# Twelve small loads around the last weights of a decode step, and w4 in two pieces instead of eight, begun after the last projection

## The chip, the cores and the metric

The kernel runs on one core of one Trainium2 chip. The metric is device time in microseconds (us) of one execution; lower is better. Times inside an execution are counted from its first instruction.

## The reference

One token goes through two blocks and the results are added. Block A is attention with 32 query heads over 4 key/value heads of 65536 cached keys each. Block B is a small MLP.

```python
xn = layernorm(x)
# A: 134 MB of cache are read once
q = xn @ wq                                    # 1024 x 4096
o = softmax(q @ K^T * 128**-0.5) @ V           # per head, K and V: [4, 65536, 128]
A = o @ wo                                     # 4096 x 1024
# B
h  = gelu(layernorm(xn) @ w1);  x1 = xn + shifted(h) @ w2
B  = x1 + gelu(layernorm(x1) @ w3) @ w4        # w4: 3584 x 1024
out = x + A + B
```

All is bf16. Some 170 MB have to come from memory for very little arithmetic, so the kernel is a race against its own loads. The shifts leave only zeros at a sequence length of one.

## The kernel before

Loads go through one queue (SyncE) into three slots of 64 KB per partition, in a fixed order. The last four are the last K tile, wo, the last V tile, and w4. A slot is loaded again when its user is done.

```python
SLOTS = 3
W4_PIECES = (6, 5, 6, 4, 3, 2, 1, 1)         # in chunks of 128 rows; 28 in all
...
for u in range(NU):
    if u == NU - 1: stream += [("K", u), "wo", ("V", u)]
    else:           stream += [("K", u), ("V", u)]
stream.append("w4")
...
elif it == "w4":
    w4_v = B_w4.rearrange("(m c) n -> m c n", c=FC)
    c0 = 0
    for n in W4_PIECES:
        go(out=t[:, c0 * D:(c0 + n) * D], in_=w4_v[:, c0:c0 + n, :].rearrange("p c n -> p (c n)"))
        c0 += n
```

Everything that forms the output row is added up in one PSUM tile, `psB`. Its two halves of 512 columns sit in two column groups of the PE array, so two matmuls (a pair) run at a time: both start within 7 ns and take 0.38 us each at full clock. The end of the program is:

```python
def compute_w4(lo, hi):
    for c in range(lo, hi):
        for j in range(2):                    # one pair for each chunk
            row_acc(j, hT[:, c:c + 1], wt[:, D * c + 512 * j:D * c + 512 * (j + 1)])
...
for g in range(HKV - 1): project(g)           # o @ wo for three heads groups
add_projection()                              # ... copied (o_rows) and added into psB
compute_v(NU - 1)                             # last P @ V; then on DVE: og, ol; PE: pm_e; DVE: oT
early = sum(W4_PIECES[:2])                    # 11 chunks
compute_w4(0, early)
project(HKV - 1)                              # 8 pairs, needs oT
compute_w4(early, FC)
# out_t <- psB, store
```

Between the last V matmul and `oT` there is a chain of small steps on DVE with one matmul (`pm_e`) in it. Apart from four matmuls that add `o_rows`, PE has nothing else to do there but the early w4 matmuls.

## Time and profile before

| | before |
|---|---|
| time, median of 2 runs | 402.12 us |
| span of the profiled run | 400.3 us |
| last V tile landed | 379.3 us |
| last piece of w4 landed | 396.7 us |
| PE done with psB | 397.2 us |

The page of the kernel before, its span, the busy time of the engines, its load queue (packets, MB, share of 16 DMA engines) and what was read:

```profile
span 400.3 us, 2563 instructions
...
PE 236.0 (59%) x1348; PEld 45.2 (11%) x854; DVE 208.9 (52%) x154; ACT 27.3 (7%) x35; POOL 5.3 (1%) x28
...
q1 hardware_dynamic: 4560, 169.87, 98.6%
...
HBM read 169.87 MB, written 0.00 MB: 424 GB/s over the span
```

The DMA engines are busy all the time; no compute engine is. The chain of waits of the kernel before, its end (start us, us, what):

```profile
379.33 17.39 DMA big<-in_B_w_dram
396.73 0.04 issue
396.77 0.40 PE psB L191 x2
397.17 0.02 issue
397.19 0.58 ACT out_t L455
```

After the last byte of w4 only one pair of matmuls is left. The timeline of PE in the kernel before shows why (start us, us, engine, line, op, out<-in, shapes, count, then in brackets the idle time and what ended it; rows of other engines are left out):

```profile
386.21 2.30 PE L191 MATMUL psB<-big,hT 128*1 128x512 bf16 x10
...
388.44 0.80 PE L403 MATMUL pm_e<-ol,sel8big 128*128 128x129 f32 x2
...
389.17 1.50 PE L191 MATMUL psB<-big,hT 128*1 128x512 bf16 x12
...
390.51 1.89 PE L191 MATMUL psB<-big,oT 128*1 128x512 bf16 x16
...
392.23 2.97 PE L191 MATMUL psB<-big,hT 128*1 128x512 bf16 x26
395.47 1.03 PE L191 MATMUL psB<-big,hT 128*1 128x512 bf16 x6 [0.27 <-DMA big<-in_B_w_dram]
...
396.77 0.38 PE L191 MATMUL psB<-big,hT 128*1 128x512 bf16 x2 [0.27 <-DMA big<-in_B_w_dram]
```

The first two rows of w4 (10 and 12 matmuls) are the early ones; 16 with oT are the last projection. From 395.47 PE waits for the loads, so it has caught up. Ten matmuls from 386.21 take 2.30 us; 26 later take 2.97 us. The cause is PE's granted clock, in the busy times by stretch (us; busy time and count of PE, PEld, DVE, ACT, POOL; granted clock; DMA share and GB/s):

```profile
384.00:386.00 2.00, 0.88 (x4) 0.09 (x4) 1.97 (x3) 0.00 (x0) 0.00 (x0) 0.97 1.03 426
386.00:389.30 3.30, 3.30 (x16) 1.08 (x16) 1.52 (x3) 0.00 (x0) 0.00 (x0) 0.50 0.99 417
389.30:393.00 3.70, 3.70 (x36) 1.44 (x34) 0.91 (x4) 0.00 (x0) 0.00 (x0) 1.00 1.00 412
```

PE was idle for 1.33 us before its four `o_rows` matmuls at 385.12; the clock records show 0.50 from 385.88 to 389.29. So the early matmuls themselves run at half clock, and the last projection, from 390.51, has the full clock. A pair starts every 0.425 us at 0.50 and every 0.2155 us at 1.00. The clock records change in steps of 3.41 us.

### The profile page before, as it was taken

The numbers are of one execution on the slowest core, as the hardware profiler recorded it, in microseconds if no ns is written. First come the engines' busy times: TensorE is split into PE (matmuls) and PEld (weight loads), VectorE is DVE, ScalarE is ACT, GpSimd is POOL, SyncE is SP. The second block draws the span as 40 slices with busy tenths as digits, with TensorE's granted clock in tenths as the row PEclk, the third lists the DMA queues.
The fourth block names the chain that finished last, engine by engine and source line by source line (L and its number), as shares of the span: only waits on it lengthen the run. The fifth ranks groups of instructions, "written<-read, shape, count | busy, mean of one in ns | idle before, by whom it ended". The sixth has DMA issues, their size and how long they took to land.

```text
span 400.3 us, 2563 instructions
## 1 busy us (share of the span) xinstructions
PE 236.0 (59%) x1348; PEld 45.2 (11%) x854; DVE 208.9 (52%) x154; ACT 27.3 (7%) x35; POOL 5.3 (1%) x28
## 2 busy tenths in 40 slices
PE   0561960591678247922965195629453946594986
PEld 0210000010200110011102010201020102000222
DVE  1601010965196549644953994279349931975040
ACT  1001010003000200020002000100100020002000
POOL 2000000000000000000000000000000000000000
PEclk9995795597669666978796789568865986697989
DMA  9998999999999999999999999999999998999895
GB/s 419 419 453 371 435 471 458 426 419 419 421 426 465 452 426 414 426 426 432 445 460 426 419 426 419 447 439 452 426 421 426 432 445 385 432 481 426 385 417 201
DMA packets 4575, 170.01 MB, mean 425 GB/s; under 512 B 467, under 2 KB 469, under 8 KB 982
## 3 DMA queue, kind: packets, MB, share of 16 engines
q1 hardware_dynamic: 4560, 169.87, 98.6%
q8 instruction: 8, 0.13, 0.1%
q14 instruction: 1, 0.01, 0.0%
q10 hardware_dynamic: 6, 0.00, 0.0%
HBM read 169.87 MB, written 0.00 MB: 424 GB/s over the span
## 4 chain that ended last, share of the span: by engine, by line
DMA 51%; DVE 26%; PE 16%; ACT 3%; another core or an unknown queue 2%; issue 1%; DVEq 0%; ACTq 0%
DMA big<-in_A_k_cache_dram 31%; DVE big L327 19%; DMA big<-in_A_v_cache_dram 10%; PE sc L332 8%; PE oacc L382 6%; DMA big<-in_A_wq_dram 6%; DMA big<-in_B_w_dram 4%; DVE p_sb L353 3%; DVE mx L337 3%; ACT p_sb L350 3%; PE psq L257 2%; DVE m L341 0%; PE pm_mx L339 0%; PE pm_mx L346 0%
## 5 line engine op out<-in xcount | busy, mean ns | idle before, releaser
L332 PE MATMUL sc<-big,qdiag 128*128 128x512 bf16 x512 | 129.5, 414 | 62.7 <-DVE big L327 57.2
L327 DVE STREAM_TRANSPOSE big<-big 128x4096 f32<-128x4096 f32 x32 | 139.4, 4413 | 49.4 <-DMA big<-in_A_k_cache_dram 49.4
L382 PE MATMUL oacc<-big,p_sb 128*32 128x512 bf16 x512 | 46.9, 539 | 34.5 <-DVE p_sb L353 34.5
L337 DVE TENSOR_REDUCE mx<-sc 128x1 f32<-128x2048 f32 x8 | 18.3, 2291 | 30.0 <-PE sc L332 30.0
L332 PEld LDWEIGHTS <-qdiag 128*128 128x128 bf16 x128 | 13.2, 103 | 174.7 <-issue 145.9
L350 ACT ACTIVATE p_sb<-sc,nball 128x2048 bf16<-128x2048 f32 x8 | 15.7, 1967 | 217.8 <-DVE nball L348 217.8
L353 DVE STREAM_TRANSPOSE p_sb<-p_sb 128x2048 bf16<-128x2048 bf16 x8 | 18.5, 2311 | 18.0 <-ACT p_sb L350 18.0
L382 PEld LDWEIGHTS <-p_sb 128*32 128x32 bf16 x512 | 17.1, 129 | 61.0 <-DVE p_sb L353 35.1
L257 PE MATMUL psh<-big,ln_rep_b 128*32 128x512 bf16 (+1 forms) x64 | 12.4, 941 | 7.6 <-DMA big<-in_B_w_dram 7.6
L421 PE MATMUL o_acc<-big,oT 128*1 128x512 bf16 x48 | 12.8, 437 | 2.4 <-ACT p_sb L350 2.4
L339 PE MATMUL pm_mx<-ident_f,mx 128*1 128x128 f32 x8 | 2.2, 273 | 19.1 <-DVE mx L337 19.1
L296 DVE STREAM_TRANSPOSE h_row<-h_row 128x896 bf16<-128x896 bf16 x1 | 1.1, 1111 | 20.8 <-ACT h_row L295 20.8
L391 DVE SCALAR_TENSOR_TENSOR og<-oacc,wb,og 128x512 f32<-128x512 f32 x4 | 3.0, 746 | 16.7 <-PE oacc L382 16.7
L191 PE MATMUL psB<-big,hT 128*1 128x512 bf16 x56 | 8.1, 424 | 0.6 <-DMA big<-in_B_w_dram 0.5
L427 DVE COPY o_rows<-o_acc 1x1024 f32<-1x1024 f32 x1 | 1.2, 1211 | 13.6 <-PE oacc L382 13.6
L205 PE MATMUL pm_ln<-ln_rowsum_a,ones_f 128*128 128x1 f32 x2 | 0.6, 348 | 12.5 <-DVE ln_rowsum_a L203 12.5
L403 PE MATMUL pm_e<-ol,sel8big 128*128 128x129 f32 x8 | 2.8, 446 | 7.9 <-DVE ol L402 7.9
L257 PE MATMUL psq<-big,ln_rep_a 128*32 128x512 bf16 x64 | 6.2, 573 | 1.5 <-DMA big<-in_A_wq_dram 1.5
L281 POOL COPY qdiag<-qx 32x32 bf16<-32x32 bf16 x16 | 3.2, 203 | 279.5 <-PE sc L332 249.6
L196 DVE STREAM_TRANSPOSE x_t<-x_row 32x256 bf16<-32x256 bf16 x4 | 2.5, 616 | 8.1 <-DMA x_row<-in_A_x_dram 8.0
L269 DVE CAST q_row<-psq 128x512 bf16<-128x512 f32 x1 | 0.7, 691 | 8.4 <-PE psq L257 8.4
L346 PE MATMUL pm_mx<-ident_f,rep 1*128 1x1 f32 x8 | 1.8, 223 | 5.0 <-DVE rep L343 5.0
(95 smaller groups left out, 73.2 us busy)
## 6 DMA issues: line engine op xcount, KB each, us to landing
big<-in_A_wo_dram SPq DMA_DIRECT2D x1, 8192.0 KB, 36.0
big<-in_B_w_dram SPq DMA_DIRECT2D x1, 7168.0 KB, 38.3
big<-in_B_w_dram SPq DMA_DIRECT2D x2, 2048.0 KB, 46.3
big<-in_B_w_dram SPq DMA_DIRECT2D x2, 1536.0 KB, 27.3
big<-in_B_w_dram SPq DMA_DIRECT2D x1, 1280.0 KB, 24.1
big<-in_B_w_dram SPq DMA_DIRECT2D x1, 1024.0 KB
big<-in_B_w_dram SPq DMA_DIRECT2D x1, 768.0 KB, 30.7
big<-in_B_w_dram SPq DMA_DIRECT2D x1, 512.0 KB, 31.5
```

The lines of the kernel that those rows point to most:

```text
L191: nc.tensor.matmul(psB[32 * j:32 * j + lhsT.shape[1], :], lhsT=lhsT, rhs=rhs, start=start, stop=False, tile_position=(0, 32 * j), skip_gro ...
L257: nc.tensor.matmul(acc[32 * q:32 * q + 32, i, 0:n], lhsT=rep[:, c, :], rhs=cols(c, i, q), start=(c == 0), stop=(c == DC - 1), tile_positio ...
L281: nc.gpsimd.tensor_copy(out=qdiag[at, LEAD:].rearrange("p (x c) -> p x c", x=4)[:, :, 32 * a:32 * a + 8], in_=qx[at, :, 8 * g:8 * g + 8])
L327: nc.vector.transpose(out=words, in_=words)
L332: nc.tensor.matmul(sc[:, e, :], lhsT=qdiag[:, c0:c0 + P], rhs=cols[:, s, e, :, b2, :, r], start=(s == 0 and b2 == 0 and r == 0), stop=(s = ...
L337: nc.vector.reduce_max(out=mx[:], in_=sc[:].rearrange("p e n -> p (e n)"), axis=AX.X)
L350: nc.scalar.activation(out=p_sb[:], in_=sc[:], func=ACTF.Exp, bias=nball[:, b:b + 1], scale=SCALE, accum_out=group["lall"][:, b:b + 1])
L353: nc.vector.transpose(out=flat, in_=flat)
L382: nc.tensor.matmul(oacc[32 * q:32 * (q + 1), :], lhsT=pT[:, e, 32 * t:32 * (t + 1)], rhs=vt[:, :, e, t, :], start=(e == 0 and t < 4), stop ...
L391: nc.vector.scalar_tensor_tensor(out=og[:], in0=oacc[:], scalar=wb[:, 1:2], in1=og[:], op0=ALU.mult, op1=ALU.add)
L403: nc.tensor.matmul(pe[:, 0:DH + 1], lhsT=sel8big[:], rhs=ol[:], start=True, stop=True)
L421: nc.tensor.matmul(tail["rows"][0:1, h2, :], lhsT=oT[g][:, j:j + 1], rhs=wt[:, g, j, 512 * h2:512 * (h2 + 1)], start=(g == 0 and j == 0), ...
```

## The change

Six small loads stand behind wo, and six between two pieces of w4. Each has k rows of 16k bytes, with its own k, into a small tile that nobody reads. No two have the same size, so they can be told apart in the packet records; we take them for marks that show how far each DMA engine has come. With that w4 comes in two pieces, 20 and 8 chunks, and none of it is worked on before the last projection.

```diff
-W4_PIECES = (6, 5, 6, 4, 3, 2, 1, 1)
+W4_PIECES = (20, 8)
+FIRST_MARKS = (3, 6, 8, 10, 13, 15)
+MARKS = (4, 5, 7, 9, 11, 14)
...
+            if it == "wo":
+                marks, m0 = ogpool.tile([P, D], BF16, name="marks", tag="og"), 0
+                self.marks = marks
+                for k in FIRST_MARKS:
+                    go(out=marks[0:k, m0:m0 + 8 * k], in_=A_wo[0:k, 0:8 * k])
+                    m0 += 8 * k
...
                 for n in W4_PIECES:
                     go(...)
+                    if c0 == 0:
+                        marks, m0 = self.marks, 440
+                        for k in MARKS:
+                            go(out=marks[0:k, m0:m0 + 8 * k], in_=A_wo[0:k, 0:8 * k])
+                            m0 += 8 * k
                     c0 += n
...
-    early = sum(W4_PIECES[:2])
+    early = 0
```

So three things change at once: the small loads, the pieces, and the order on PE.

More of the change, by code (lines that the diff above doesn't have):

```diff
@@ L153, in load @@
                     go(out=t[:, c0 * D:(c0 + n) * D], in_=w4_v[:, c0:c0 + n, :].rearrange("p c n -> p (c n)"))
+                    if c0 == 0:
[3 more added lines that the diff above has]
+                            m0 += 8 * k
                     c0 += n
-            else:
+            elif it[0] in ("K", "V"):
                 kind, i = it
```

## The prediction

> **What bounds the kernel now.** The loads. The page gives a mean of 425 GB/s over the 400.3 us span, one queue busy for 98.6% of 16 engines, HBM read 169.87 MB; PE is busy 59%, DVE 52%. The chain of waits ends with a V-cache load that lands at 379.3, 17.39 us of loading w4, then 0.40 us of two psB matmuls, 0.58 us of ACT out_t and the store. w4 comes in eight pieces, the last of one chunk, so almost no PE work follows the last byte. PE has caught up with the loads by then.
>
> **Removed.** Six of the eight w4 loads. The bytes stay. In the trace's packet records a 2048-byte packet takes 84 ns and a 65536-byte one 2418 ns, so by estimate each packet costs about 9 ns beyond its bytes; 54 packets fewer per DMA engine save about 0.5 us before the last w4 byte lands.
>
> **Added.** Twelve loads of k rows and 16k bytes. [...] Estimate: 20 to 30 ns each[...].  Each takes about 0.35 us to issue on SP, off the path. In the changed build, DMA semaphores are reused every eight loads: the last V load now waits for K to land (near 340.5 instead of 338.8), the second w4 piece for V (379.3). At both moments another load still has over 10 us to run, so I expect no bubble.
>
> **Moved: the part that matters.** PE did 11 chunks of w4 before the last projection. Now the order on PE is: V matmuls (end 383.8), o_rows, pm_e, 16 projection matmuls, 40 matmuls of w4 when 20 chunks have landed (estimate 379.3 + 17.4 x 20/28 = 391.7), 16 for the last 8 chunks. pm_e no longer queues behind w4, so oT is ready near 389.5 (390.2 before). PE idles for most of 384 to 389.5 and its granted clock will be 0.50 there; the timeline shows a pair of these matmuls 0.43 us apart at 0.50 and 0.216 us at 1.00. [...] this trace's clock records step in 3.41 us. So the projection's 8 pairs start cold, and the clock returns between 391.3 and 396. From 389.5, 36 pairs then end between 398.2 and 400.4, mean about 399.3, against 397.17 before. Even without cold clock, 16 matmuls (1.7 us) follow the last landing instead of two (0.4).
>
> **On the critical path:** +1.0 to +3.3 us in the tail, about +2.1; loads -0.3 to +0.1. Predicted 404.2 us, 403.1 to 405.5 (8 in 10); faster by over 2%: 0.01, within 2%: 0.97, slower by over 2%: 0.02.
>
> **What would show it.** Right: the rate stays near 425 GB/s until the last w4 byte, which lands within 0.5 us of 396.7; the chain's end shows 2 to 4 us of psB matmuls instead of 0.4; PE mostly idle 384 to 389 at clock 0.50; runs scatter more than before. Wrong: a DMA gap behind the small loads or before the second w4 piece; V landing later by over 0.5 us.
>
> **What would make me wrong.** [...]a bubble from the semaphore waits, would add microseconds; a clock that returns early would keep the loss to 1 us.

The forecast's sum came to 404.2 us: 402.1 for the kernel before, about 2.1 more in the tail, and -0.3 to +0.1 for the loads. At most 0.3 us for the small loads, half of it before V lands, went into the term for the loads. Its 20 to 30 ns for each load is the estimate from the packet records: 9 ns for a packet beyond its bytes, 9 ns for a packet of 4 bytes that goes with it, and a few for the bytes. The range of 391.3 to 396 for the clock's return is the estimate from the steps of 3.41 us.

## The result, and the profile after

The changed kernel took 403.78 us (403.70 to 403.86, 2 runs), against 402.12 before. The ratio is 1.004, with a 95% interval of 1.002 to 1.006. Ratios here are the mean time of one kernel's fast runs over that of the other's of the same rounds, so not quite the ratio of the medians that are quoted. Executions over 1.5% slower than the fastest of the same kernel are left out of the means. Later the same kernel took 403.69 to 405.02, median 404.90, 5 runs, ratio 1.006 (1.0047 to 1.0072). All seven runs together have a median of 404.09. 31 runs of the kernel before lie between 401.96 and 402.29. All differences here are below 2%; they are clear of the noise all the same.

The end of the chain of waits of the changed kernel (first profile):

```profile
379.58 17.01 DMA big<-in_B_w_dram
396.60 0.04 issue
396.64 1.91 PE psB L204 x16
398.55 0.02 issue
398.57 0.58 ACT out_t L468
```

The last byte lands 0.13 us earlier than before (396.60 against 396.73), but 16 matmuls follow instead of 2: 1.91 us instead of 0.40. PE ends at 398.55 instead of 397.17, 1.38 us later. (The median times differ by 1.66 us; the other 0.3 us come after PE's end and are not explained here.) The timeline of PE in the changed kernel, same profile:

```profile
387.07 0.49 PE L416 MATMUL pm_e<-ol,sel8big 128*128 128x129 f32 x2 [1.42 <-DVE ol L415]
...
388.63 3.22 PE L204 MATMUL psB<-big,oT 128*1 128x512 bf16 x16 [1.06 <-DVE oT L425]
...
391.76 4.48 PE L204 MATMUL psB<-big,hT 128*1 128x512 bf16 x40
...
396.64 1.89 PE L204 MATMUL psB<-big,hT 128*1 128x512 bf16 x16 [0.40 <-DMA big<-in_B_w_dram]
```

And the stretches of the changed kernel, with the same columns as before:

```profile
384.00:386.00 2.00, 1.02 (x4) 0.09 (x4) 1.93 (x3) 0.00 (x0) 0.00 (x0) 1.00 0.87 369
386.00:389.30 3.30, 1.16 (x6) 0.52 (x8) 1.96 (x5) 0.00 (x0) 0.00 (x0) 0.79 1.00 432
389.30:393.00 3.70, 3.70 (x26) 1.26 (x24) 0.00 (x0) 0.00 (x0) 0.00 (x0) 0.72 0.94 385
```

PE is now idle where the early w4 matmuls were (1.16 us busy against 3.30), and the half clock lies on the projection: 16 matmuls take 3.22 us instead of 1.89. In this execution the clock came back at 391.4, early enough to finish 40 matmuls before the last piece landed. The second profile of the same kernel (run e10 below) was less lucky. Its chain has no load at the end at all:

```profile
388.95 10.77 PE psB L204 x72
399.72 0.02 issue
399.75 0.58 ACT out_t L468
```

There the clock records show 0.50 from 387.4 to 394.3, and PE worked through 72 matmuls without once waiting for a load.

The loads themselves: the last V load was issued at 340.68 (338.78 before), the second piece of w4 at 379.58, when V had landed. In the packet records 16 or more packets are under way at every moment from 338 to 384 us, and the profile counts 16 engines, so we take it that no engine ran dry there. Six small packets in a row (11 to 18 ns each), each with a packet of 4 bytes and 9 ns that we take for its semaphore write, took 95 to 100 ns, some 16 ns for each load. That they are of one engine is read from their order in time.

### The profile page after: what moved, and what is told of

Same layout as the page of the kernel before. It is cut to its first block, busy times and chain, and to the rows that moved or that the text cites. A ratio compares the mean times of both kernels' runs of the same rounds, so it can differ in the third digit from the quotient of the medians.

```text
span 401.8 us, 2570 instructions
## 1 busy us (share of the span) xinstructions
PE 230.6 (57%) x1348; PEld 44.9 (11%) x854; DVE 209.0 (52%) x154; ACT 27.3 (7%) x35; POOL 5.4 (1%) x28
## 4 chain that ended last, share of the span: by engine, by line
DMA 61%; DVE 19%; PE 14%; ACT 2%; another core or an unknown queue 2%; issue 1%; DVEq 0%; ACTq 0%; SPq 0%
DMA big<-in_A_k_cache_dram 42%; DVE big L340 14%; DMA big<-in_A_v_cache_dram 10%; PE sc L345 7%; DMA big<-in_A_wq_dram 5%; PE oacc L395 4%; DMA big<-in_B_w_dram 4%; DVE p_sb L366 2%; DVE mx L350 2%; ACT p_sb L363 2%; PE psq L270 1%; PE psB L204 0%; PE pm_mx L352 0%; DVE m L354 0%
## 5 line engine op out<-in xcount | busy, mean ns | idle before, releaser
L395 PE MATMUL oacc<-big,p_sb 128*32 128x512 bf16 x512 | 43.1, 511 | 34.5 <-DVE p_sb L366 34.5
L204 PE MATMUL psB<-big,hT 128*1 128x512 bf16 x56 | 6.4, 379 | 0.4 <-DMA big<-in_B_w_dram 0.4
```

What stands on the lines that cost most here:

```text
L204: nc.tensor.matmul(psB[32 * j:32 * j + lhsT.shape[1], :], lhsT=lhsT, rhs=rhs, start=start, stop=False, tile_position=(0, 32 * j), skip_gro ...
L395: nc.tensor.matmul(oacc[32 * q:32 * (q + 1), :], lhsT=pT[:, e, 32 * t:32 * (t + 1)], rhs=vt[:, :, e, t, :], start=(e == 0 and t < 4), stop ...
```

## The experiments

Two theories stood at the start. One: the loss is the 16 matmuls that follow the last landing. The rival: the small loads cost it. The first results made a third one necessary: the loss is the cold clock on the work left when the early matmuls are gone. All kernels gave correct results. The runs are told by theme and not in order of their numbers; there are no runs e5 to e7. The kept traces of e9, e10, e11 and e12 come from a second profile of each; lines below are of the first one unless the text says "second profile".

### e1: no small loads

```diff
 (the kernel before)
-W4_PIECES = (6, 5, 6, 4, 3, 2, 1, 1)
+W4_PIECES = (20, 8)
-    early = sum(W4_PIECES[:2])
+    early = 0
```

> The changed kernel without any of the twelve small loads: w4 in two pieces (20, 8), w4 not begun before the last projection. Theory (the loss is the 16 matmuls that now follow the last landing): about 1.4 to 1.7 us above before, so 403.5 to 403.9 us, the small loads being worth 0.1 to 0.2 us at most; the chain ends with some 1.9 us of psB matmuls. Rival (the small loads cost it): within 0.3 us of before.

Measured: 403.53 us (403.30 to 404.10, 5 runs), ratio 1.0039 (1.0027 to 1.0051). The loss is there without a single small load. But the chain does not end as the first theory said. The chain of e1, at its end (the profile is of the slowest run):

```profile
389.53 9.57 PE psB L191 x72
399.10 0.02 issue
```

PE was late by itself: the clock records show 0.50 from 386.0 to 392.8.

### e2: the small loads alone

```diff
 (the changed kernel)
-W4_PIECES = (20, 8)
+W4_PIECES = (6, 5, 6, 4, 3, 2, 1, 1)
-    early = 0
+    early = sum(W4_PIECES[:2])
```

> The kernel before plus the twelve small loads alone (the eight pieces of w4 and the early w4 matmuls stay; the second six stand behind the first piece). Theory: 402.0 to 402.5 us[...]; the chain ends with 0.4 us of psB matmuls. Rival: 403.5 us or more. The later w4 pieces now also wait for earlier pieces' semaphores; if a DMA gap shows between w4 pieces it is this, not the small packets.

Measured: 402.78 us (402.25 to 403.77, 5 runs), ratio 1.0021 (1.0009 to 1.0033). This is more than expected, and the profile (of the slowest run) shows the side effect that the expectation named. Loads take turns on eight semaphores in these traces, and a load that reuses one waits until the load eight places before it has landed. With six loads in between, the third piece of w4 waits for the first one (SyncE waited 3.3 us for it, and 15.2 us for the last V load before the second piece). The chain of e2 goes through the load queue's issues:

```profile
383.25 0.35 SPq L161
...
384.60 0.58 SPq L161
385.18 0.04 issue
385.23 1.12 SPq L161
```

The pieces reached the queue just when it ran empty (the first packets of the second and third piece took 0.7 to 1.2 us, where 0.39 and 0.46 are usual), and the last one landed at 397.99 instead of 396.73. In the changed kernel there are two pieces, and this does not happen. So e2 does not measure the packets; it shows that small loads that do little harm beside two pieces can cost more beside eight.

### e3: a short last piece in the changed kernel

```diff
 (the changed kernel)
-W4_PIECES = (20, 8)
+W4_PIECES = (20, 7, 1)
```

> The changed kernel, all small loads kept, its last piece of 8 chunks cut into 7 and 1. Theory: the last landing is then followed by two matmuls (0.4 us) in place of 16 (1.9 us), but PE work of 28 chunks after the 20-chunk piece lands near 391.6 takes 6.0 us at full clock, so PE ends near 397.6 to 397.8: about 0.8 us below the changed kernel, near 403.0. Rival (small loads): as the changed kernel, 403.7.

Measured: 404.14 us (402.91 to 404.50, 5 runs), ratio 1.004 (1.0027 to 1.0053). A miss, but for one run at 402.91: no gain, although only one pair now follows the last landing. In its profile the clock came back at 393.3, and PE worked from 389.74 to 399.41 without a wait. This fells the first theory as the whole cause. The 16 matmuls are a floor under the end; where PE is late by itself, what decides is how long it works at half clock.

### e4: only the order

```diff
 (the kernel before)
-    early = sum(W4_PIECES[:2])
+    early = 0
```

> The kernel before with the eight pieces, but no w4 matmul before the last projection (early = 0). Theory: PE stands idle to 388.6, starts cold, and has 36 pairs to do; it catches up with the loads late, ending 0.2 to 0.9 us after before: 402.3 to 403.0. If order were the whole cause of the loss: 403.7. If order did not matter at all: 402.1.

Measured: 403.95 us (402.68 to 404.56, 6 runs), ratio 1.0042 (1.003 to 1.0054), well above the expected 402.3 to 403.0. One line of the change, the one that adds no load and no work, brings a loss as large as the whole. And it brings the scatter: 1.9 us where the kernel before has 0.3. The stretches of e4:

```profile
386.00:389.30 3.30, 1.32 (x8) 0.55 (x10) 1.79 (x5) 0.00 (x0) 0.00 (x0) 0.75 0.98 412
389.30:393.00 3.70, 3.70 (x20) 1.17 (x18) 0.00 (x0) 0.00 (x0) 0.00 (x0) 0.50 1.00 412
```

Between 389.3 and 393 PE was fully busy at half clock, where the kernel before had 1.00.

### The sum behind it

From the start of the last projection PE has 36 pairs to do (8 of wo, 28 of w4). If the clock comes back at W and the projection starts at s, then (W - s) / 0.425 pairs are done cold and the rest takes 0.2155 us a pair. The last matmul ends 0.17 us after its slot. This is worked out from numbers of the traces alone; W is read from their clock records:

| profile | s | W | worked out | PE ends in the chain |
|---|---|---|---|---|
| e1 | 389.53 | 392.8 | 399.07 | 399.10 |
| e3 | 389.74 | 393.3 | 399.42 | 399.41 |
| e4 | 388.47 | 394.5 | 399.37 | 399.38 |
| e10, changed kernel again | 388.95 | 394.3 | 399.74 | 399.72 |
| e10, second profile | 388.86 | 392.15 | 398.41 | 398.42 |
| e14, below | 389.04 | 392.0 | 398.43 | 398.44 |
| changed kernel, first profile | 388.63 | 391.4 | 397.92 | 398.55 |

In e10's first profile the clock came back to 0.95 only; the view of the stretch from 394.3 to 399.7 has 48 matmuls in 5.40 us, 0.225 us a pair, and that is used there, so this row is a weaker check than the others. In the last row PE was done with the 20 chunks in time and the floor applies: landing at 396.60 plus 1.95 us is 398.55. So the end is the later of the two, the work and the floor. In e14 and in e10's second profile the two nearly fall together: their last bytes landed at 396.49 and 396.42, so the floors are 398.44 and 398.37.

### e10: the changed kernel again

No edit.

> The changed kernel itself again, for its scatter and its median over more runs. Theory now (cold clock: from the start of the last projection near 388.5 PE works through 36 pairs at 0.425 us a pair[...], then at 0.2155 us; the landing of the last piece plus 1.9 us is only the floor): runs between 403.3 and 404.6 us, scattered by over 0.5 us, mean near 403.8. Rival (16 matmuls after the landing are all of it): all runs within 0.3 us of each other.

Measured: 404.90 us (403.69, 404.09, 404.90, 404.96, 405.02). The scatter of 1.3 us is what the cold clock predicts, and not what a fixed tail of 16 matmuls would give. The two profiles of e10 show it: with the clock back at 394.3 PE ended at 399.72, with the clock back at 392.15 at 398.42. The upper end is 0.4 us above what was expected.

### e11 and e12: fill PE's idle time

If the clock is the cause, matmuls of no use in the idle time must take the loss away. They read the last V tile and write a PSUM tile that nobody reads. e11 has them in e1, e12 has them in e4:

```diff
+        if u == NU - 1:
+            idle = ps_M.tile([P, 512], F32, name="idle", tag="pm")
+            for c in range(11):
+                for j in range(2):
+                    nc.tensor.matmul(idle[32 * j:32 * j + 1, :], lhsT=hT[:, c:c + 1],
+                                     rhs=st.tiles[("V", u)][:, 512 * (2 * c + j):512 * (2 * c + j + 1)],
+                                     start=True, stop=True, tile_position=(0, 32 * j), ...)
         st.done(("V", u))
```

> The changed kernel without the small loads, with 22 matmuls of no use (they read the last V tile, write a PSUM tile that nobody reads) that fill PE's idle time between the V matmuls and pm_e, 11 on each side of o_rows; 1.2 us of fill on each side at full clock. Clock theory: the clock stays at 1.00, the tail is set by the last landing plus 16 matmuls: 403.3 to 403.6 us, runs within 0.3 us. Rival (clock is not it): as without the filler, 403.3 to 404.1 and scattered, or slower for 22 matmuls more.

Measured e11: 403.44 us (403.13 to 403.49, 5 runs), ratio 1.003 (1.0017 to 1.0043). The scatter is gone (0.36 us), and the clock records show 1.00 from 372.0 to 402.8 (second profile). What is left is the floor of 16 matmuls after the landing, in the chain of e11:

```profile
362.32 33.93 DMA big<-in_B_w_dram
...
396.29 1.91 PE psB L191 x16
```

> The kernel before with early = 0 (which alone gave 403.95 us, 402.68 to 404.56) and the same 22 filling matmuls. Clock theory: warm from 388.5 on, the 36 pairs end at 388.5 + 7.8 = 396.3 before the last piece lands, so the loss vanishes: 402.0 to 402.4 us, scatter under 0.3 us. Rival (the order itself costs it: 11 chunks not done early): 403 us or more.

Measured e12: 402.36 us once, 403.53 to 403.62 four times; ratio 1.0028 (1.0014 to 1.0042). A miss in four runs of five, but not for the rival's reason. The timeline of PE in e12:

```profile
388.69 1.89 PE L191 MATMUL psB<-big,oT 128*1 128x512 bf16 x16 [1.06 <-DVE oT L419]
390.41 6.07 PE L191 MATMUL psB<-big,hT 128*1 128x512 bf16 x54
398.18 0.38 PE L191 MATMUL psB<-big,hT 128*1 128x512 bf16 x2 [1.70 <-DMA big<-in_B_w_dram]
```

PE was warm, done early, and waited 1.70 us for the last piece, which landed at 398.14. The page of e12 has one instruction fetch more than the eight of the kernel before:

```profile
q8 instruction: 9, 0.15, 0.1%
```

The packet records have it at 395.92, 16384 bytes, 1.12 us. We take it to come with the program's length, 44 PE instructions more: the pages of e11 and e12, which have them, show nine fetches, those of e13 and e14, with 13 more, eight. That it held up one DMA engine's share of the last piece fits the times, but is inferred. In the second profile the ninth fetch stands at 395.98 and delayed nothing: the last piece landed at 396.69. PE had full clock throughout and never waited for a load, as the chain of that profile shows:

```profile
389.61 7.95 PE psB L191 x72
397.57 0.02 issue
```

Its span is 400.7 us, where the kernel before has 400.2 to 400.5. So with the clock up the loss was nearly gone here, although PE began its 36 pairs late, at 389.61.

### e13 and e14: a leaner filler

Eleven matmuls in one column group with one weight load, 13 PE instructions (count from the build). e13 has them in e4, e14 in the changed kernel.

```diff
-                for j in range(2):
-                    nc.tensor.matmul(idle[32 * j:32 * j + 1, :], lhsT=hT[:, c:c + 1], ...
+                nc.tensor.matmul(idle[0:1, :], lhsT=hT[:, 0:1], rhs=st.tiles[("V", u)][:, 512 * c:512 * (c + 1)],
+                                 start=True, stop=True, tile_position=(0, 0), ...)
```

> The kernel before with early = 0 and a leaner filler: 11 matmuls in one column group with one weight load, so 13 PE instructions more in place of 44. In the run with 22 matmuls the clock stayed at 1.00 and PE waited 1.70 us for the last piece, but a ninth 16 KB instruction fetch took a DMA engine for 1.12 us at 395.9, just ahead of its share of that piece, and four of five runs took 403.5 to 403.6, one 402.36. Theory (cold clock is the loss, the fetch an accident of program length): without the ninth fetch 402.0 to 402.4 us in all runs; the trace shows eight fetches. Rival (order costs it even when warm): 403 us or more with eight fetches.

Measured e13: 402.20, 402.32, 402.88, 403.41, 403.88, 404.21 us; median 403.15, ratio 1.0026 (1.0012 to 1.004). A miss in four runs of six, and the rival's 403 or more in three. The profile is of the run at 402.20. It has eight fetches and a clock of 1.00 from 370.2 to 400.9. Its timeline of PE:

```profile
388.29 1.89 PE L191 MATMUL psB<-big,oT 128*1 128x512 bf16 x16 [1.06 <-DVE oT L417]
390.01 5.35 PE L191 MATMUL psB<-big,hT 128*1 128x512 bf16 x48
395.59 1.01 PE L191 MATMUL psB<-big,hT 128*1 128x512 bf16 x6 [0.23 <-DMA big<-in_B_w_dram]
396.86 0.38 PE L191 MATMUL psB<-big,hT 128*1 128x512 bf16 x2 [0.26 <-DMA big<-in_B_w_dram]
```

With the clock up, the kernel with early = 0 waits for the loads at its end like the kernel before, in the same time. In this execution, then, the order itself cost nothing. The other runs have no profile; that the thinner filler did not hold the clock in them is argued, not shown. Their mean granted clock (0.800 to 0.805 in the four slower runs, 0.808 and 0.812 in the two others) fits, but the kernel before has 0.795 to 0.817 without any loss. And the two slowest, 404.21 and 403.88, are 2.4 us above their spans where the others are 1.8 above, so 0.6 us of them lies outside the span.

> The changed kernel, small loads and all, with the lean filler of 11 matmuls. Theory: clock at 1.00, tail set by the last landing plus 16 matmuls, the small loads worth under 0.2 us: 403.2 to 403.7 us, runs within 0.4 us of each other (the changed kernel alone: 403.69 to 405.02; with filler and without small loads 403.13 to 403.49). Rival (the small loads cost something of their own): 403.8 or more.

Measured e14: 403.64 us (403.61 to 403.78, 5 runs), ratio 1.0039 (1.0026 to 1.0052). In its profile the clock did drop, from 388.6 to 392.0, one step only, so the theory of a clock at 1.00 missed; it cost nothing, as PE's own work ended with the floor (398.44). The scatter is 0.2 us. The mean is 0.35 us over that of e11, and 0.24 us of that is the later landing (396.49 against 396.25).

### e8: a try at beating both

```diff
 (the kernel before)
-W4_PIECES = (6, 5, 6, 4, 3, 2, 1, 1)
+W4_PIECES = (11, 10, 5, 1, 1)
-    early = sum(W4_PIECES[:2])
+    early = sum(W4_PIECES[:1])
```

> A try at beating both: the kernel before with w4 in five pieces (11, 10, 5, 1, 1), the first 11 chunks worked on before the last projection. Three pieces fewer are 24 packets fewer per DMA engine at about 9 ns each (estimate from 84 ns for 2048 bytes against 2418 ns for 65536): 0.2 us earlier landing, 401.8 to 402.1 us. If packets cost nothing beyond bytes: 402.1.

Measured: 402.15 us (402.10 to 402.27, 5 runs), ratio 1.0001 (0.9989 to 1.0013). No gain. In its chain the last wait is for the piece of 5 chunks, at 395.22, and 14 matmuls (1.69 us) follow. The saving in packets is there all the same: the last byte landed at 396.51 and PE ended at 396.95, both 0.22 us earlier than in the kernel before (396.73 and 397.17), and the output followed as much earlier. Yet both spans are 400.3 us; where the 0.2 us go after the output has landed is open. No version here beats the kernel before.

### e9 and e15: all twelve small loads behind wo

```diff
 (the changed kernel)
-FIRST_MARKS = (3, 6, 8, 10, 13, 15)
-MARKS = (4, 5, 7, 9, 11, 14)
+FIRST_MARKS = (3, 6, 8, 10, 13, 15, 4, 5, 7, 9, 11, 14)
+MARKS = ()
```

> The changed kernel with all twelve small loads behind wo, none between the pieces of w4. A load waits for the load eight before it (they share a semaphore), so the eighth small load now waits for wo to land (near 360) and the last V load, behind it in the queue, is issued after that, near 362. Theory: the DMA engines run dry there for about 3 us; 406 to 407.5 us. If only the count and bytes of small loads mattered: as the changed kernel, 403.8.

Measured: 408.88, 408.90 and 409.43 us in fast runs, and one slow execution at 461.83 in which the first profile fell; ratio of the fast runs 1.0173 (1.0157 to 1.0188). The sign is right, the size (some 5 us) is above the 406 to 407.5 expected. e15 is the same kernel, for a better profile:

> The kernel with all twelve small loads behind wo once more, for a profile in the fast state (the first fell in a slow execution at 461 us; its fast runs took 408.9 to 409.4). Theory: the last V load is issued some 5 us after wo has landed at 360, no bytes move between; if the semaphore wait is not it, V is issued near 341 as before.

Measured: 409.80 us, one run (state unknown). The waits of its load queue (line 155 is the small loads), and its stretches:

```profile
SPq L155 <- DMA big<-in_A_wo_dram: 19.3, 1, 19.3
...
358.00:360.00 2.00, 2.00 (x11) 0.28 (x3) 0.00 (x0) 0.00 (x0) 0.00 (x0) 1.00 0.27 109
360.00:362.00 2.00, 1.85 (x9) 0.10 (x1) 0.11 (x1) 0.00 (x0) 0.00 (x0) 1.00 0.02 2
```

A small load waited 19.3 us for wo to land, and the last V load behind it was issued at 361.79 instead of 340.68. For some 3.5 us almost nothing was moved. The second profile of e9 (span 407.4 us) shows the same, with V issued at 361.71; there the last byte of w4 landed at 402.15, over 5 us later than in the changed kernel, and why that is more than the gap is open. So twelve small loads cost a few tenths of a microsecond as six and six, and some 5 us as twelve in a row.

## Why the prediction was right, point by point

- **What bounds the kernel: right.** The loads do; before and after, V lands near 379.4 and w4 near 396.6.
- **Fewer pieces land earlier by about 0.5 us: right.** Without small loads, two pieces landed at 396.25 and 396.40 (e11, e1), eight at 396.73 to 396.88 (before, e4, e13): 0.3 to 0.6 us.
- **Small loads: right in sign, the estimate for each load too high.** Some 16 ns, not 20 to 30. The records show k packets of 16k bytes for each load, and agree with one semaphore write for each of them (210 packets more than in e1, and the k of the twelve loads add up to 105); they do not name the engines. V landed at 379.39 to 379.57 in the five kept profiles with small loads at two places, and at 379.16 to 379.48 in the seven without: about 0.15 us by the means, though the ranges overlap. Why it is that much is open.
- **No bubble from semaphore waits: right** for the changed kernel, for both waits that were named. e2 and e15 show how close it was.
- **PE idle from 384 to 389 at clock 0.50: half right.** It was idle (1.02 of 2.00 us and 1.16 of 3.30 us busy), but in the first profile the clock was 1.00 until 387.95, and the half clock fell on the projection.
- **Early w4 matmuls gone, projection cold, tail longer: right, and one of two causes.** e4 has it alone, the second profile of e12 and that of e13 show nearly nothing of the loss when the clock stays up. The other is the 16 matmuls after the last landing, which the text named too (1.7 us, measured 1.91); e11 has it alone. In the first profile, of the run at 403.70, this floor set the end: the cold work alone would have ended at 397.92. So the text gave its weight to the path that did not decide there; the first profile of e10 is decided by it.
- **When the clock returns.** The text gave 391.3 to 396. The profiles of kernels with early = 0 and no filler have 391.4, 392.2, 392.8, 393.3, 394.3 and 394.5. The mean end of PE was set at 399.3; it was 398.55 in the first profile and 399.72 and 398.42 in the two of e10. The two first runs, at 403.78, were at the lucky end; all seven have a median of 404.09, where 404.2 was predicted.
- **oT near 389.5: too late by up to 1.1 us.** It was ready at 388.4 to 389.7 by profile.
- **"2 to 4 us of psB matmuls" at the chain's end: mis-sized.** The first profile has 1.91 us, the floor; those in which PE is late by itself have its whole run since the projection, 9.4 to 10.9 us.
- **Runs scatter more: right.** 1.3 us in seven runs against 0.3 us in 31.

My own first theory in the experiments, that 16 matmuls after the landing were all of it, was worse than the prediction; e3 and e4 felled it. The size of the parts: the seven runs of the changed kernel have a mean of 404.32, some 2.2 us above the kernel before. Some 1.2 us are the floor (e11's mean of 403.34 less 402.14) and some 0.35 us come with the small loads (e14 less e11). What is left, 0.6 us in the mean and up to 1.3 by run, is the half clock. So in the mean the floor is the larger part, and the half clock makes the scatter.

## What to carry to other kernels

Matmuls that look free because they hide under a load may keep PE busy enough to bring its clock back (here it was back at 389.29 with 22 of them, at 391.4 to 394.5 in the profiles without them and without filler); before moving them, count the work left after the next wait at half clock (0.425 us a pair here), not at full clock (0.2155). When runs of one kernel begin to scatter, put the clock records beside the end of the chain: two profiles of the same code can end in different limits (the changed kernel at 398.55 by the last landing, at 399.72 by the half clock). Count semaphores too: a tiny load can hold back a large one behind it in its queue if it reuses the semaphore of a load that hasn't landed (in e15 the last V load went out at 361.79 instead of 340.68).

## What the traces show of the clock, the fetches and the small loads

- In the traces of the kernel before and of the changed kernel all edges of the clock records lie on one grid of 3.41 us each, and the two grids lie differently (edges at 385.88 and 389.29 before, at 387.95 and 391.36 after). PE busy for 2.73 of 3.41 us brought the clock back in the changed kernel (387.95 to 391.36), 2.60 us in e4 did not (387.66 to 391.07). Over all fourteen kept traces, 407 steps of 3.41 us at half clock were followed by another one, with PE busy for 2.61 us at most, and 250 were followed by the full clock, with 2.61 us or more, but for one with 2.38. In the traces of before and after alone, 30 and 28 were followed by another one, with 2.48 and 2.05 us at most, and 18 each by the full clock, with 3.28 and 2.69 us or more.
- The first profile of e10 shows a granted clock of 0.95 where the others have 1.00 (0.225 us a pair instead of 0.2155), and the slow execution of e9 shows 0.56 in every stretch that was read.
- A fetch's packet of 16384 bytes takes 0.99 to 1.10 us in the traces of before and after, the ninth one in e12's first profile 1.12 us. It stands just before the last weights, which landed at 398.14; in the second profile the ninth delayed nothing (396.69).
- A small load inside a full queue cost some 16 ns: six took 95 to 100 ns in a row.
